# Heads' results kept features by tokens, with 32x32 turns on VectorE in place of TensorE's transposes

## The chip, the cores and the metric

One core of one Trainium2 chip. The metric is the device time of one execution in microseconds; lower is better. The kernel before has a median of 2641.17 us over three runs (2639.9 to 2641.59). Its profiled execution took 2642.54 us, of which the trace's span is 2640.5 us.

## The reference

x is 2048 tokens by 576 features in fp32. It is normalised, goes through an attention with 32 heads of 18 features and through a gated network with 4608 hidden units; the two results are multiplied and added to x.

```python
xn = _layernorm(x, axis=-1)
q, k, v = ...            # from xn @ wqkv, each heads x tokens x 18
scores = jnp.einsum("bhqd,bhkd->bhqk", q, k) * Dh ** -0.5
o = jnp.einsum("bhqk,bhkd->bhqd", softmax(scores), v)
s = o.transpose(0, 2, 1, 3).reshape(B, S, D) @ wo
gate, up = xn @ W_gate, xn @ W_up
g = silu(((gate * (gate > 0)) * up) @ W_down)
return x + s * g
```

## The kernel before

Most products are made in split fp32: each operand is a rounded high part and a low part, and three products are added. The contraction of these products uses 64 rows of TensorE at a time, so that two of them, on the upper and the lower 64 rows ("lanes"), run side by side. The class `Lanes` keeps a plan of both lanes, of eight PSUM banks and of VectorE ("V") and ScalarE ("A"), with fixed costs in microseconds, and hands out the matmuls in the order in which this plan would run them. A score matmul takes a bank when the plan has one free (`room`, `take`); `evict` books the bank's emptying on V or A; `hold` takes a bank for something else and `pause` moves both lanes on. TensorE's instructions keep that order; the other engines get theirs from the framework.

There are three stages.

- **Start** (to about 420 us): normalisation, q, k and v; the first hidden units.
- **Main loop** (about 420 to 2560 us): for each pair of heads `u` (16) four cycles `i`. A cycle runs two hidden units (`pg`, `pu`, `py`: gate, up, down), 32 score matmuls `psx` whose exponentials go through ScalarE, and 32 matmuls `pm` of the next pair of heads, whose row maxima VectorE takes (L383). Then `attend` multiplies 64 times with the values (`po`). After an odd cycle the two halves of `po` are added into `ot` (L855) and the pair of token halves is finished.
- **Projection** (last 80 us): for 16 tiles of 128 tokens, `heads` splits the attention's result into high and low parts, 28 matmuls `pw` multiply with `wo`, VectorE multiplies with the gate (L1046), GpSimd adds x (L1050), and SyncE stores.

Two things in the main loop are turned round by TensorE. `max_rows` (every 128x64 block of maxima `mx`) makes 128x32 values `nx` (maximum as high and low part), transposes them into a bank, copies them to `nt` on ScalarE and writes them with 8 DMAs as two extra rows into the q tiles `qT`, where the exponentials' matmuls subtract them. `finish_pair` (features on partitions: 18 of each 32 are a head's results, the 19th is the sum of its exponentials) transposes `ot` in four 128x128 blocks into a bank, after which VectorE takes the reciprocals `rc` (L786), multiplies into `ob` (L788, twice), and one DMA stores to `od`, tokens by features. Both wait in the list `tasks` until after the next even cycle's `attend`. In the projection `heads` transposes each tile of `od` back, in five 128x128 blocks (`tps`), so that features are on partitions; ScalarE and VectorE read these from PSUM (L991 to L997).

GpSimd meanwhile splits the weights (`gw`, `dw`, L295 and L296), in the projection it multiplies the gate (L971). All loads and stores of these stages go through SyncE's queue (SP), in the order in which the framework puts them.

Of the kernel before, what the change touches and what calls it, by code (L numbers as in the profile page):

```python
# [9 lines left out]
F32 = mybir.dt.float32  # L10
F32R = mybir.dt.float32r
AF = mybir.ActivationFunctionType
ALU = mybir.AluOpType
# [194 lines left out]
def kernel(  # L208
# [26 lines left out]
    HW = 2 * DH  # L235
# [3 lines left out]
    KA = 3 * DH  # L239
    C4 = 4 * P  # L240
    DT = D - C4
# [19 lines left out]
    def tp(*args):  # L261
        return keep(nc.tensor.transpose(*args))  # L262
# [20 lines left out]
    lanes = Lanes(8, bank, mm, fence)  # L283
# [62 lines left out]
    tasks = []  # L346
# [281 lines left out]
    two = pool(right, "two", 2, "right")  # L628
# [118 lines left out]
    def place_v(u):  # L747
        if u < NU:
            va, raw = vas[u % 2], raws.pop(u)
            for i in range(2):  # L750
                keep(nc.gpsimd.tensor_copy(va[:, :, i * VA : i * VA + DH], raw[:, :, i * DH : (i + 1) * DH]))

    def run_tasks(todo):
        for fn, args in todo:
            fn(*args)

    def max_rows(qs, mx):

        nm = two.tile([P, 2, 2, 4], F32, name="nm")
        nx = two.tile([P, 2, 2, 2, 4], F32, name="nx")  # L760
        nc.vector.tensor_reduce(nm, mx, axis=AX.X, op=ALU.max, negate=True)
        nxr = nx.bitcast(F32R)
        nc.scalar.activation(nxr[:, :, :, 0], nm, AF.Copy)
        nc.vector.tensor_tensor(nxr[:, :, :, 1], nm, nx[:, :, :, 0], ALU.subtract)
        b, ps = lanes.hold("tp")
# [3 lines left out]
        def write(ps):  # L769
            nc.scalar.activation(nt_.bitcast(F32R), ps[0:32, 0:P], AF.Copy)  # L770
            for q, qT in enumerate(qs):
                for h in range(2):
                    for a in range(2):
                        r = h * R + KA + a
                        p0 = q * 16 + h * 8 + a * 4
                        nc.sync.dma_start(
                            qT[r : r + 1, :].rearrange("o (j t) -> o j t", t=P).bitcast(F32), nt_[p0 : p0 + 4, :]
                        )

        lanes.evict(b, ps, lanes.pause(0.2), [("A", 0.27, write)])  # L780

    def finish_pair(ot, dst, then, *args):

        def write(ps):
            rc = two.tile([P, 16], F32, name="rc")
            nc.vector.reciprocal(rc, ps.rearrange("p (a d) -> p a d", d=32)[:, :, DH])  # L786
            for q in range(2):
                nc.vector.tensor_tensor(  # L788
                    dst[q].rearrange("p t (h d) -> p t h d", d=DH),
                    ps.rearrange("p (t h q d) -> p q t h d", h=2, q=2, d=32)[:, q, :, :, :DH],  # L790
                    rc.rearrange("p (t h q) -> p q t h", h=2, q=2)[:, q].unsqueeze(3).to_broadcast([P, 4, 2, DH]),
                    ALU.mult,
                )
            then(*args)

        def rest_():
# [36 lines left out]
    def attend(u, qp, done):  # L833
# [22 lines left out]
            done(qp, ot)  # L856

        lanes.evict(b, ps, end, [("V", 0.69, add)] if ots else [("A", 0.6, copy)])

    def to_dram(u):  # L860
        ob = two.tile([P, NT, HW], F32, name="ob", bufs=1)

        def store(qp):
            ts = slice(qp * NT // 2, (qp + 1) * NT // 2)
            nc.sync.dma_start(od[:, u * HW : (u + 1) * HW].rearrange("(t p) d -> p t d", p=P)[:, ts], ob[:, ts])

        return lambda qp, ot: finish_pair(
            ot, [ob[:, (2 * qp + q) * 4 : (2 * qp + q + 1) * 4, :] for q in range(2)], store, qp
        )

    def cycle(k, scores):

# [28 lines left out]
    for k in range(0, N1, 2):  # L901
        i = k // 2
# [15 lines left out]
    for u in range(NU):  # L918
        done = to_dram(u)
        pms = [maxima(u + 1, h) if u + 1 < NU else deque() for h in range(2)]  # L920
        for i in range(UN // 2):
# [9 lines left out]
            qp, k0 = i // 2, i % 2 * (NT // 2)  # L931
# [16 lines left out]
    fo = pool(fin, "fo", 4)  # L948
# [32 lines left out]
    def any_bank(name):  # L981
        turns[0] += 1
        return bank(turns[0] % 8, name)

    def heads(o):

        ps = any_bank("tps")
        for c in range(4):
            tp(ps[:, c * P : (c + 1) * P], o[:, c * P : (c + 1) * P], ident)
        hh = hp.tile([P, 2, 512], F32R, tag="hh", name="hf", bufs=4)  # L990
        nc.scalar.activation(hh[:, 0], ps, AF.Copy)  # L991
        nc.vector.tensor_tensor(hh[:, 1], ps, hh[:, 0].bitcast(F32), ALU.subtract)
        p5 = any_bank("tps")
        tp(p5[:, :P], o[:, C4:], ident)
        o5 = f2.tile([P, P], F32R, name="o5")
        nc.scalar.activation(o5, p5[:, :P], AF.Copy)
        nc.vector.tensor_tensor(o5[DT:P], p5[DT:P, :P], o5[DT:P].bitcast(F32), ALU.subtract)  # L997
# [15 lines left out]
    for j in range(4):  # L1013
        js = slice(j * P, (j + 1) * P)
        for n in range(2):
            cs = halves[n]
            ps = any_bank("py")[:, :HC]
# [5 lines left out]
    run_tasks(tasks)  # L1023
# [56 lines left out]
```

## Time and profile before

| | us | share of the span |
|---|---|---|
| median of three runs | 2641.17 | |
| profiled execution | 2642.54 | |
| its span | 2640.5 | 100% |
| TensorE matmuls busy | 2607.2 | 99% |
| VectorE busy | 1733.0 | 66% |
| ScalarE busy | 1464.0 | 55% |
| GpSimd busy | 1442.1 | 55% |
| transposes of `ot`, TensorE, 128 of 273 ns (overlapping) | 492.9 to 2566.7 | |
| transposes of `o` in the projection, 80 of 272 ns (overlapping) | 2566.9 to 2624.2 | |

PE is TensorE, PEld its weight loads, DVE VectorE, ACT ScalarE, POOL GpSimd, SP SyncE. Matmuls overlap in the pipeline, so the time that a group takes is read from the starts of what stands before and behind it, not from the durations. The granted TensorE clock is 1.00 in every stretch from 280 us on but the last 10.5 us (0.97).

### The profile page before, as it was taken

The page shows a single profiled execution, that of the slowest core. Times are in us where ns is not written, and L with a number is a line of the kernel's source. Part 1 is how long each engine was busy: PE and PEld are TensorE (multiplying, and loading weights), DVE is VectorE, ACT ScalarE, POOL GpSimd, SP SyncE. Part 2 cuts the span into 40 slices and gives each one's busy share as a digit, 9 for nine tenths or more (in the row PEclk, how much of TensorE's full clock was granted, in tenths as well). Part 3 has the DMA queues.
Part 4 walks back from the last instruction along what each step waited for, and adds up shares of the span by engine and source line. Part 5 has one row for each costly group of instructions (what it writes and reads, how often), then busy time and mean ns, then how long its engine had stood idle before and what let it go on. Part 6 is the DMA issues. An engine that isn't in the chain of part 4 may idle for free.

```text
span 2640.5 us, 62759 instructions
## 1 busy us (share of the span) xinstructions
PE 2607.2 (99%) x25436; PEld 2119.1 (80%) x25436; DVE 1733.0 (66%) x2888; ACT 1464.0 (55%) x2755; POOL 1442.1 (55%) x1273
## 2 busy tenths in 40 slices
PE   7998999999999999999999999999999999999999
PEld 5997887778887777777778778887777777778789
DVE  5325557777777777777777777777777777776124
ACT  2221226666666666666666666666666666666662
POOL 5234886555555555555555555555555555555555
PEclk9998999999999999999999999999999999999999
DMA  8644332222232222222242222222233222222247
GB/s 253 201 145 147 88 87 74 71 69 72 83 115 72 67 70 73 74 73 74 69 132 63 67 75 66 75 71 72 73 99 89 70 76 70 74 66 56 59 123 237
DMA packets 293265, 243.69 MB, mean 92 GB/s; under 512 B 64496, under 2 KB 236272, under 8 KB 292976
## 3 DMA queue, kind: packets, MB, share of 16 engines
q1 hardware_dynamic: 286192, 216.08, 28.2%
q0 software_dynamic: 6784, 23.60, 2.8%
q8 instruction: 201, 3.29, 0.5%
q14 instruction: 88, 0.72, 0.1%
HBM read 193.45 MB, written 45.61 MB: 91 GB/s over the span
## 4 chain that ended last, share of the span: by engine, by line
PE 93%; DMA 2%; POOL 2%; SPq 1%; DVE 1%; ACT 0%; issue 0%; POOLq 0%; ACTq 0%; DVEq 0%
PE pg L259 22%; PE po L259 17%; PE py L259 16%; PE pu L259 11%; PE pm L259 9%; PE psx L259 9%; PE pq L259 4%; PE pv L259 2%; PE pw L259 1%; PE tp L262 1%; SPq L353 1%; PE tps L262 1%; DMA rg<-in_B_W_up_dram 1%; DMA kT<-kd 1%; DMA gt<-yd 0%; DMA out_dram<-xr 0%
## 5 line engine op out<-in xcount | busy, mean ns | idle before, releaser
L383 DVE TENSOR_REDUCE mx<-pm 128x1 f32<-128x512 f32 x2048 | 1379.1, 689 | 254.4 <-PE pm L259 168.5
L817 ACT ACTIVATE p<-psx 128x512 f32<-128x512 f32 x2048 | 1182.3, 598 | 542.1 <-PE psx L259 258.8
L259 PE MATMUL pg<-x,gw 64*128 64x512 f32 x3888 | 1159.7, 392 | 5.7 <-POOL gw L296 3.7
L259 PE MATMUL pu<-x,gw 64*128 64x512 f32 x3888 | 1146.9, 392 | 0.0
L259 PE MATMUL pm<-kT,qT 54*128 54x512 f32 x2048 | 794.1, 398 | 3.0 <-DMA kT<-kd 3.0
L259 PE MATMUL psx<-qT,kT 56*128 56x512 f32 x2048 | 786.3, 394 | 0.0
L259 PEld LDWEIGHTS pg<-x,gw 64*128 64x128 f32 x3888 | 721.0, 187 | 60.5 <-POOL gw L296 4.6
L259 PEld LDWEIGHTS pu<-x,gw 64*128 64x128 f32 x3888 | 718.9, 187 | 25.0
L259 PE MATMUL py<-dw,hh 64*128 64x288 f32 x6864 | 717.5, 295 | 1.4 <-POOL dw L296 0.3
L259 PEld LDWEIGHTS py<-dw,hh 64*128 64x128 f32 x6864 | 662.8, 186 | 49.3 <-issue 30.1
L259 PE MATMUL po<-p,va 128*32 128x512 f32 x4096 | 452.7, 594 | 0.4 <-ACT p L817 0.4
L667 POOL CAST hh<-h 128x512 fp32r<-128x512 f32 x127 | 77.6, 611 | 612.3 <-DVE h L664 612.3
L694 POOL TENSOR_TENSOR y<-yt,y 128x288 f32<-128x288 f32 x268 | 215.2, 806 | 323.7 <-ACT yt L693 323.5
L259 PEld LDWEIGHTS psx<-qT,kT 56*128 56x128 f32 x2048 | 375.3, 185 | 18.9
L296 POOL TENSOR_TENSOR gw<-rg,gw 128x1152 fp32r<-128x1152 f32 x144 | 383.5, 2664 | 11.6
L259 PEld LDWEIGHTS pm<-kT,qT 54*128 54x128 f32 x2048 | 372.4, 185 | 18.5 <-issue 3.2
L259 PEld LDWEIGHTS po<-p,va 128*32 128x32 f32 x4096 | 126.4, 110 | 279.1 <-issue 269.1
L296 POOL TENSOR_TENSOR dw<-rd,dw 128x576 fp32r<-128x576 f32 x144 | 204.9, 1423 | 11.5
L670 POOL TENSOR_TENSOR hh<-h,hh 128x512 fp32r<-128x512 f32 x144 | 186.3, 1294 | 38.0 <-ACT hh L669 27.8
L295 POOL CAST gw<-rg 128x1152 fp32r<-128x1152 f32 x144 | 165.2, 1147 | 18.0 <-DMA rg<-in_B_W_up_dram 11.5
L689 DVE TENSOR_TENSOR y<-py,y 128x288 f32<-128x288 f32 x268 | 120.2, 449 | 49.5 <-PE py L259 48.9
L660 ACT ACTIVATE h<-pg 128x512 f32<-128x512 f32 x144 | 85.9, 597 | 116.7 <-PE pg L259 56.2
(80 smaller groups left out, 1353.0 us busy)
## 6 DMA issues: line engine op xcount, KB each, us to landing
rd<-in_B_W_down_dram SPq DMA_DIRECT2D x144, 288.0 KB
rg<-in_B_W_gate_dram SPq DMA_DIRECT2D x144, 256.0 KB
rg<-in_B_W_up_dram SPq DMA_DIRECT2D x144, 256.0 KB
qT<-qd SPq DMA_DIRECT2D x384, 36.0 KB
kT<-kd SPq DMA_DIRECT2D x384, 36.0 KB
kd<-hh POOLq DMA_DIRECT2D x16, 512.0 KB, 4.6
qd<-hh POOLq DMA_DIRECT2D x16, 512.0 KB, 5.7
xTd<-x SPq DMA_DIRECT2D x15, 512.0 KB
```

What stands on the lines that cost most here:

```text
L259: return keep(nc.tensor.matmul(*args, **kw))
L262: return keep(nc.tensor.transpose(*args))
L295: keep(nc.gpsimd.tensor_copy(hi, raw))
L296: keep(nc.gpsimd.tensor_tensor(lo, raw, hi.bitcast(F32), ALU.subtract))
L353: nc.sync.dma_start(dst[r0 : r0 + DH, :].bitcast(F32), src[i, f0 : f0 + DH, cs])
L383: nc.vector.tensor_reduce(mx[:, g % 2, h, j, c : c + 1], ps, axis=AX.X, op=ALU.max)
L660: nc.scalar.activation(made[0], ps, AF.Relu)
L667: keep(nc.gpsimd.tensor_copy(hh[:, 0], h))
L670: keep(nc.gpsimd.tensor_tensor(hh[:, 1], h, hh[:, 0].bitcast(F32), ALU.subtract))
L689: nc.vector.tensor_tensor(ys[j][:, cs], ps[:, :HC], ys[j][:, cs], ALU.add)
L694: keep(nc.gpsimd.tensor_tensor(ys[j][:, cs], t, ys[j][:, cs], ALU.add))
L817: nc.scalar.activation(p[0][:, h, i, :], ps, AF.Exp, scale=SCALE)
```

## The change

The heads' results stay features by tokens: `od` is now 576 x 2048. `to_dram` gives a `finish` that runs directly behind the add of the two halves: a 32x32 block transpose of `ot` on VectorE brings each block's 32 features onto the free axis, the reciprocals and the product are made there in place, a second block transpose turns the blocks back, and four DMAs store 18 rows of 512 tokens each. `max_rows` turns its 128x32 values in the same way, stores them to a small DRAM tile `nd`, and four DMAs read them back as rows. The plan no longer holds banks or pauses for these; it books 1.9 us on V for a finished pair, and 1.2 us on V and 0.25 us on A for the maxima. In the projection `load_heads` loads features by tokens, and `heads` splits straight from SBUF. TensorE transposes nothing but the normalised x in the start.

```diff
-    od = dram.tile([S, D], F32, name="od")
+    od = dram.tile([D, S], F32, name="od")
+    nd = dram.tile([2, 32, P], F32, name="nd")
...
-        b, ps = lanes.hold("tp")
-        tp(ps[0:32, 0:P], nx.rearrange("p q h a j -> p (q h a j)"), ident)
-        nt_ = two.tile([32, P], F32, name="nt")
...
-            nc.scalar.activation(nt_.bitcast(F32R), ps[0:32, 0:P], AF.Copy)
...
-        lanes.evict(b, ps, lanes.pause(0.2), [("A", 0.27, write)])
+        nt_ = two.tile([P, 32], F32, name="nt")
+        nc.vector.transpose(nt_, nx.rearrange("p q h a j -> p (q h a j)"))
+        lanes.server["V"] += 1.2
+        lanes.server["A"] += 0.25
+        n_ = nd[rows_kept[0] % 2]
+        rows_kept[0] += 1
+        nc.sync.dma_start(n_.rearrange("c (b t) -> b c t", b=4), nt_)
+        for q, qT in enumerate(qs):
+            for h in range(2):
+                r, p0 = h * R + KA, q * 16 + h * 8
+                nc.sync.dma_start(
+                    qT[r : r + 2, :].bitcast(F32), n_[p0 : p0 + 8, :].rearrange("(a j) t -> a (j t)", a=2)
+                )
-    def finish_pair(ot, dst, then, *args):
...
-            b, ps = lanes.hold("tp2")
-            for j in range(4):
-                tp(ps[:, j * P : (j + 1) * P], ot[:, j * P : (j + 1) * P], ident)
-            lanes.evict(b, ps, lanes.pause(0.6), [("V", 0.85, write)])
-        tasks.append((rest_, ()))
+    def to_dram(u):
+        def finish(qp, ot):
+            oT = two.tile([P, 512], F32, name="oT", bufs=1)
+            o3 = oT.rearrange("p (k d) -> p k d", d=32)
             rc = two.tile([P, 16], F32, name="rc")
+            nc.vector.transpose(oT, ot)
+            nc.vector.reciprocal(rc, o3[:, :, DH])
+            nc.vector.tensor_tensor(
+                o3[:, :, :DH], o3[:, :, :DH], rc.unsqueeze(2).to_broadcast([P, 16, DH]), ALU.mult
+            )
+            nc.vector.transpose(ot, oT)
+            lanes.server["V"] += 1.9
+            for h in range(2):
+                for i in range(2):
+                    s_ = 32 * (2 * h + i)
+                    f0, t0 = (2 * u + h) * DH, (2 * qp + i) * 512
+                    nc.sync.dma_start(od[f0 : f0 + DH, t0 : t0 + 512], ot[s_ : s_ + DH, :])
...
-        o = fo.tile([P, D + DT], F32, name="o")
-        nc.sync.dma_start(o[:, :D], od[k * P : (k + 1) * P, :])
-        nc.sync.dma_start(o[:, D:], od[k * P : (k + 1) * P, C4:])
+        o = fo.tile([P, 5, P], F32, name="o")
+        ks = slice(k * P, (k + 1) * P)
+        nc.sync.dma_start(o[:, :4], od[:C4, ks].rearrange("(c p) t -> p c t", p=P))
+        for d in range(2):
+            nc.sync.dma_start(o[d * DT : (d + 1) * DT, 4], od[C4:, ks])
...
-        ps = any_bank("tps")
-        for c in range(4):
-            tp(ps[:, c * P : (c + 1) * P], o[:, c * P : (c + 1) * P], ident)
+        o4 = o.rearrange("p c t -> p (c t)")[:, :512]
         hh = hp.tile([P, 2, 512], F32R, tag="hh", name="hf", bufs=4)
-        nc.scalar.activation(hh[:, 0], ps, AF.Copy)
-        nc.vector.tensor_tensor(hh[:, 1], ps, hh[:, 0].bitcast(F32), ALU.subtract)
+        nc.scalar.activation(hh[:, 0], o4, AF.Copy)
+        nc.vector.tensor_tensor(hh[:, 1], o4, hh[:, 0].bitcast(F32), ALU.subtract)
...
-        nc.vector.tensor_tensor(o5[DT:P], p5[DT:P, :P], o5[DT:P].bitcast(F32), ALU.subtract)
+        nc.vector.tensor_tensor(o5[DT:P], o[DT:P, 4], o5[DT:P].bitcast(F32), ALU.subtract)
```

What this does to the order of instructions is shown at three places. First VectorE, where an odd cycle of the main loop ends. Before:

```order
L761 TENSOR_REDUCE nm<-mx 128x16
L764 TENSOR_TENSOR nx<-nm,nx 128x4x4
L855 TENSOR_TENSOR ot<-po,ot 128x512
L383 TENSOR_REDUCE mx<-pm 128x1 x8
L689 TENSOR_TENSOR y<-py,y 128x288
```

And now (its line numbers are the changed kernel's):

```order
L767 TENSOR_TENSOR nx<-nm,nx 128x4x4
L769 STREAM_TRANSPOSE nt<-nx 128x32
L855 TENSOR_TENSOR ot<-po,ot 128x512
L789 STREAM_TRANSPOSE oT<-ot 128x512
L790 RECIPROCAL rc<-oT 128x16
L791 TENSOR_TENSOR oT<-oT,rc 128x16x18
L794 STREAM_TRANSPOSE ot<-oT 128x512
L384 TENSOR_REDUCE mx<-pm 128x1 x6
```

Four instructions now stand between the add and the first maximum of the next cycle; the reciprocal and two products that came one cycle later are gone from there.

Second TensorE, in the cycle behind that same place. Before, from the last product of attention on:

```order
L259 MATMUL po<-p,va_2826 32x512 x32
L259 MATMUL py<-dw,hh 128x288 x10
L259 MATMUL psx<-qT,kT_2428 128x512
L259 MATMUL pm<-kT_2436,qT 128x512
L259 MATMUL py<-dw,hh 128x288 x2
```

Now:

```order
L259 MATMUL po<-p,va_2827 32x512 x32
L259 MATMUL py<-dw,hh 128x288 x10
L259 MATMUL psx<-qT,kT_2429 128x512 x2
L259 MATMUL py<-dw,hh 128x288 x2
L259 MATMUL pg<-x,gw 128x512
L259 MATMUL pu<-x,gw 128x512
L259 MATMUL pg<-x,gw 128x512
L259 MATMUL pu<-x,gw 128x512
L259 MATMUL psx<-qT,kT_2429 128x512
L259 MATMUL pm<-kT_2437,qT 128x512
```

The plan sees VectorE taken and puts a second exponentials' matmul where the first `pm` stood; of the first 40 matmuls of 512 columns behind this place four are `pm`, where six were. Behind even cycles the five transposes are gone and the order is otherwise as it was.

Third SyncE's queue at the start of the projection. Before (`o`, `xr`, `gt` are the loads of a tile's heads, of x and of the gate's product):

```order
L968 DMA gt<-yd 128x576
L962 DMA o<-od 128x576
L963 DMA o<-od 128x64
L976 DMA xr<-in_A_x_dram 128x576
L968 DMA gt<-yd 128x576
L962 DMA o<-od 128x576
L1051 DMA out_dram<-xr 128x576
```

Now:

```order
L800 DMA od<-ot 18x512 x4
L731 DMA yd<-y 128x576 x3
L967 DMA xr<-in_A_x_dram 128x576
L959 DMA gt<-yd 128x576
L1036 DMA out_dram<-xr 128x576
L952 DMA o<-od 128x4x128
L954 DMA o<-od 64x128 x2
L967 DMA xr<-in_A_x_dram 128x576
L959 DMA gt<-yd 128x576
```

Before, the gate of tile 3 was asked for ahead of tile 0's store; now it stands behind that store, and so on for each tile: one tile less is loaded ahead. The two `gt` in each piece are those of tiles 2 and 3.

More of the change, by code (lines that the diff above doesn't have):

```diff
@@ L751, in place_v @@
                 keep(nc.gpsimd.tensor_copy(va[:, :, i * VA : i * VA + DH], raw[:, :, i * DH : (i + 1) * DH]))
+    rows_kept = [0]
     def run_tasks(todo):
@@ L764, in max_rows @@
         nc.vector.tensor_tensor(nxr[:, :, :, 1], nm, nx[:, :, :, 0], ALU.subtract)
-        b, ps = lanes.hold("tp")
-        tp(ps[0:32, 0:P], nx.rearrange("p q h a j -> p (q h a j)"), ident)
-        nt_ = two.tile([32, P], F32, name="nt")
-        def write(ps):
-            nc.scalar.activation(nt_.bitcast(F32R), ps[0:32, 0:P], AF.Copy)
[L771 to L778, printed above, removed]
@@ L780, in max_rows @@
-        lanes.evict(b, ps, lanes.pause(0.2), [("A", 0.27, write)])
-    def finish_pair(ot, dst, then, *args):
-        def write(ps):
-            rc = two.tile([P, 16], F32, name="rc")
[L786 to L796, printed above, removed]
-            b, ps = lanes.hold("tp2")
-            for j in range(4):
-                tp(ps[:, j * P : (j + 1) * P], ot[:, j * P : (j + 1) * P], ident)
-            lanes.evict(b, ps, lanes.pause(0.6), [("V", 0.85, write)])
-        tasks.append((rest_, ()))
+        nt_ = two.tile([P, 32], F32, name="nt")
@@ new lines, in to_dram @@
+    def to_dram(u):
+        def finish(qp, ot):
+            oT = two.tile([P, 512], F32, name="oT", bufs=1)
+            o3 = oT.rearrange("p (k d) -> p k d", d=32)
+            rc = two.tile([P, 16], F32, name="rc")
+            nc.vector.transpose(oT, ot)
[10 more added lines that the diff above has]
+                    nc.sync.dma_start(od[f0 : f0 + DH, t0 : t0 + 512], ot[s_ : s_ + DH, :])
+        return finish
@@ L858, in attend @@
         lanes.evict(b, ps, end, [("V", 0.69, add)] if ots else [("A", 0.6, copy)])
[L860 to L869, printed above, removed]
     def cycle(k, scores):
@@ L985, in heads @@
     def heads(o):
-        ps = any_bank("tps")
-        for c in range(4):
-            tp(ps[:, c * P : (c + 1) * P], o[:, c * P : (c + 1) * P], ident)
+        o4 = o.rearrange("p c t -> p (c t)")[:, :512]
         hh = hp.tile([P, 2, 512], F32R, tag="hh", name="hf", bufs=4)
-        nc.scalar.activation(hh[:, 0], ps, AF.Copy)
-        nc.vector.tensor_tensor(hh[:, 1], ps, hh[:, 0].bitcast(F32), ALU.subtract)
-        p5 = any_bank("tps")
-        tp(p5[:, :P], o[:, C4:], ident)
+        nc.scalar.activation(hh[:, 0], o4, AF.Copy)
+        nc.vector.tensor_tensor(hh[:, 1], o4, hh[:, 0].bitcast(F32), ALU.subtract)
         o5 = f2.tile([P, P], F32R, name="o5")
-        nc.scalar.activation(o5, p5[:, :P], AF.Copy)
-        nc.vector.tensor_tensor(o5[DT:P], p5[DT:P, :P], o5[DT:P].bitcast(F32), ALU.subtract)
+        nc.scalar.activation(o5, o[:, 4], AF.Copy)
+        nc.vector.tensor_tensor(o5[DT:P], o[DT:P, 4], o5[DT:P].bitcast(F32), ALU.subtract)
         return hh, o5
@@ L1022 @@
     store_y(last)
-    run_tasks(tasks)
     xts = {i: load_res(horder[i]) for i in range(2)}
```

## The prediction

> **What bounds the kernel now.** I read the busy shares first, then the chain of waits, then tables of stretches cut at the products of attention.
>
> ```profile
> PE 2607.2 (99%) x25436; PEld 2119.1 (80%) x25436; DVE 1733.0 (66%) x2888; ACT 1464.0 (55%) x2755; POOL 1442.1 (55%) x1273
> PE 93%; DMA 2%; POOL 2%; SPq 1%; DVE 1%; ACT 0%; issue 0%; POOLq 0%; ACTq 0%; DVEq 0%
> ...
> 459.07:485.84 26.77, 26.77 (x272) 24.80 (x268) 23.56 (x37) 20.09 (x37) 11.67 (x12) 1.00 0.24 69
> 485.84:493.50 7.66, 7.66 (x72) 2.45 (x71) 1.16 (x3) 0.86 (x3) 7.50 (x8) 1.00 0.25 68
> 493.50:520.27 26.77, 26.77 (x270) 24.47 (x269) 23.69 (x39) 20.69 (x38) 11.78 (x12) 1.00 0.27 73
> 520.27:527.27 7.00, 7.00 (x66) 1.97 (x64) 1.83 (x5) 0.81 (x3) 6.84 (x6) 1.00 0.35 96
> ```
>
> TensorE sets the end: 99% busy, 93% of the chain. The four rows are two cycles of the main loop (length; busy time of PE, PEld, DVE, ACT and POOL; clock; DMA share; GB/s). TensorE is busy in all of each row, so what leaves its queue there leaves the time, unless something new makes it wait. The third number after the length is the warning: VectorE works 23.6 of a cycle's 26.77 us. Its 66% is an average over stages; inside a cycle it is at 88%, and only during the products of attention does it rest.
>
> **What TensorE loses.** Both kinds of cycle from the start of the products of attention on:
>
> ```profile
> 452.07 7.07 PE L259 MATMUL po<-p,va 128*32 128x512 f32 x64
> 459.07 0.94 PE L259 MATMUL py<-dw,hh 64*128 64x288 f32 x10
> 459.84 0.39 PE L259 MATMUL psx<-qT,kT 56*128 56x512 f32 x1
> ...
> 485.84 7.07 PE L259 MATMUL po<-p,va 128*32 128x512 f32 x64
> 492.85 0.28 PE L262 MATMUL tp<-ident,nx 128*32 128x128 f32 x1
> 492.97 0.60 PE L262 MATMUL tp<-ident,ot 128*128 128x128 f32 x4
> 493.50 0.94 PE L259 MATMUL py<-dw,hh 64*128 64x288 f32 x10
> ```
>
> Behind an odd cycle 7.00 us pass from the first `po` to the first `py`; behind an even one, with five transposes, 7.66 us. So five transposes cost 0.66 us on TensorE, not the 1.4 us that their overlapping durations add up to. Of the 32 pairs of halves 31 are turned round in the loop: 31 x 0.66 = **20.5 us** off the path. The two sets of maxima before the loop bring 0.2 us more.
>
> **What VectorE gains, and who waits.** The finish of a pair moves from a place where VectorE rested (behind the transposes, 0.26 us of reciprocal and two products of 0.31 us) to directly behind the add of an odd cycle, where the next cycle's maxima queue up behind it. What it costs:
>
> ```profile
> L383 DVE TENSOR_REDUCE mx<-pm 128x1 f32<-128x512 f32 x2048 | 1379.1, 689 | 254.4 <-PE pm L259 168.5
> L689 DVE TENSOR_TENSOR y<-py,y 128x288 f32<-128x288 f32 x268 | 120.2, 449 | 49.5 <-PE py L259 48.9
> L786 DVE RECIPROCAL rc<-tp x32: 249/258/259, 493.6 to 2567.1; 128x16 f32<-128x16 f32 x32
> L788 DVE TENSOR_TENSOR ob<-tp,rc x64: 295/306/308, 493.9 to 2567.6; 128x144 f32<-128x144 f32 x64
> 459.21 0.69 DVE L855 TENSOR_TENSOR ot<-po,ot 128x512 f32<-128x512 f32 x1 [5.04 <-PE po L259]
> 460.30 0.69 DVE L383 TENSOR_REDUCE mx<-pm 128x1 f32<-128x512 f32 x1 [0.40 <-PE pm L259]
> 459.40 0.67 POOL L295 CAST dw<-rd 128x576 fp32r<-128x576 f32 x1
> 460.14 1.43 POOL L296 TENSOR_TENSOR dw<-rd,dw 128x576 fp32r<-128x576 f32 x1
> ```
>
> No block transpose of VectorE stands in this trace. The two group rows, 512 elements in 0.69 us and 288 in 0.45, give about 0.14 us fixed and 1.07 ns an element. If a turn passes one element a cycle it takes 0.69 us, which I use, since every fp32 pass over 512 columns here takes that; if it streams two at a time, 0.14 + 0.27 = 0.41; if it has to pass everything twice, 0.14 + 1.10 = 1.24.
>
> The product of 288 elements reads both operands from SBUF, and for that the trace shows a trap:
>
> ```profile
> 2633.02 1.43 POOL L1050 TENSOR_TENSOR xr<-xr,gt 128x576 f32<-128x576 f32 x1 [0.91 <-DVE gt L1046]
> 2633.34 1.43 DVE L1048 TENSOR_TENSOR xr<-xr,gt 128x288 f32<-128x288 f32 x1
> 2635.17 0.46 DVE L1048 TENSOR_TENSOR xr<-xr,gt 128x288 f32<-128x288 f32 x1
> ```
>
> The same instruction takes 0.46 us alone and 1.43 us when it meets GpSimd's: GpSimd's ends at 2634.45, and VectorE's, 0.32 us later, at 2634.77. It waited for GpSimd to end. [...]
>
> Now the finish, from the add's start at 459.21. Add to 459.90; first turn to 460.62; reciprocal to 460.9; then the product meets GpSimd's `dw`, which runs to 461.57, and is through at 461.9; second turn to 462.6. VectorE's first maximum starts there instead of at 460.30, 3.5 us into the cycle instead of 1.2. After that it has its old 23 us of work less 0.69 us of add, and its idle time in the cycle was 3.2 us, so the sum still fits (about 26 of 26.77). TensorE waits only where banks run out.
>
> Walk them: eight banks, four of them with the open accumulations (two `py`, `pg`, `pu`), four for scores. The changed order has its first four `pm` as 8th, 18th, 28th and 29th matmul of 512 columns. Twelve `py` take 0.92 us (ten are 0.77: 459.07 to 459.84), and two lanes of 512 columns pass in 0.234 us (the two starts below lie seven pairs apart), so they start at 1.7, 2.9, 4.1 and 4.2 us.
>
> ```profile
> 494.87 0.39 PE L259 MATMUL pg<-x,gw 64*128 64x512 f32 x1
> 496.51 0.39 PE L259 MATMUL pg<-x,gw 64*128 64x512 f32 x1
> ```
>
> The first bank is read out at 3.5 + 0.69 = 4.2 us and free just after. With one bank still held by a `psx`, the fourth `pm` waits 0.1 to 0.2 us; behind it VectorE stays late for the rest of the cycle and gives one bank each 0.69 us, so some later ones wait as well. I take **0.35 us** for a cycle. The lower end is 0, if banks happen to suffice; the upper is 1.0, from turns of 1.24 us (finish 0.5 us later still, as GpSimd's end covers the first turn's excess), a fourth `pm` 0.6 us late and some more behind it. 29 such cycles have `pm` (the last pair of heads has none to prepare): 29 x 0.35 = **10.2 us** given back, between 0 and 29.
>
> The maxima's turn (128x32) adds some 0.2 us, but it runs while TensorE is in `po` and VectorE rests; the rows are not read until a whole cycle later, 26 us, against two transfers of a few us, so their way through DRAM is hidden. SyncE waits for the first of them, but what stands behind it, the next `rg`, waits for GpSimd anyway. ScalarE loses a copy of 0.27 us, off the path. The stores are 2 KB rows instead of pieces of 144 bytes.
>
> **The projection.** TensorE's period for a tile, and what feeds it:
>
> ```profile
> 2566.48 0.60 PE L262 MATMUL tp<-ident,ot 128*128 128x128 f32 x4
> 2568.52 1.99 PE L259 MATMUL pw<-wo,hf 128*128 128x288 f32 x12
> ...
> 2602.26 0.71 PE L262 MATMUL tps<-ident,o 128*128 128x128 f32 x5
> 2602.72 1.83 PE L259 MATMUL pw<-wo,hf 128*128 128x288 f32 x12
> 2606.51 0.71 PE L262 MATMUL tps<-ident,o 128*128 128x128 f32 x5
> ...
> 2602.84 0.38 SPq L1051 DMA_DIRECT2D out_dram<-xr  x1
> 2603.31 0.38 SPq L968 DMA_DIRECT2D gt<-yd  x1
> 2607.34 0.69 ACT L970 ACTIVATE sg<-gt 128x576 f32<-128x576 f32 x1 [2.89 <-DMA gt<-yd]
> 2608.16 1.43 POOL L971 TENSOR_TENSOR gt<-gt,sg 128x576 f32<-128x576 f32 x1 [1.40 <-ACT sg L970]
> 2600.00:2610.00 10.00, 10.00 (x80) 10.00 (x79) 3.42 (x8) 2.19 (x5) 7.00 (x6) 1.00 0.91 292
> 2558.62 6.98 POOL L1006 TENSOR_TENSOR wo<-rw,wo 128x576 fp32r<-128x576 f32 x5
> L992 DVE TENSOR_TENSOR hf<-tps,hf x16: 679/691/693, 2568.2 to 2631.1; 128x512 fp32r<-128x512 f32 x16
> L997 DVE TENSOR_TENSOR o<-tps,o x16: 294/295/296, 2568.9 to 2631.8; 64x128 fp32r<-64x128 f32 x16
> ```
>
> A tile takes 4.25 us, of which the transposes are 0.46. Without them TensorE alone would need 3.79; 16 x 0.46 and the last pair's four transposes (0.4 us) would be 7.8 us. [...] The DMA share is 0.91, so a tile keeps the queues busy for 0.91 x 4.25 = 3.9 us, and `o` in rows of 512 bytes will not make that less. GpSimd's two instructions for a tile (2 x 1.43) and VectorE's two subtractions (0.69 and 0.29), which now read both operands from SBUF, exclude one another: 3.84 us. [...] I take 4.0 us, 0.25 less than now, over 13 tiles: 3.3 us.
>
> At the start the change loses some of it. VectorE does two `hf` subtractions before the last add, each behind one of GpSimd's five `wo` instructions (6.98 us in a row), and the last finish, so the first gate product, the first store and with it the gate of tile 3 come some 3 us later; TensorE itself starts its first `pw` 2 us earlier (2566.48 instead of 2568.52), since `hf` no longer waits for it. Net I count **0.5 us** gained for the stage, between 6 lost (4.5 us a tile and the late start) and 7.8 gained.
>
> **Sum**, against the profiled execution's 2642.54 us (1.4 above the median of 2641.17): -20.5 - 0.2 + 10.2 - 0.5 = -11.0, which from the median is **2630 us**.
>
> **Rivals.**
>
> *All of it arrives.* The banks suffice, or the turns take 0.41 us; the product still waits for GpSimd's 461.57, so the first maximum comes at 3.2 us. With 0.1 us a cycle and 3 us from the projection: -20.7 + 2.9 - 3 = -20.8, 2620. For it: VectorE's sum fits its cycle. Against: the fourth `pm`.
>
> [...]
>
> *VectorE becomes the bound of the main loop.* Its place is the finish, its price the turns. At 1.24 us each, 1.0 us a cycle: 29.0 given back against 20.7, and a projection 1 us worse: +9.3, 2650. It decides from 0.7 us a cycle on (20.5 / 29). For it: VectorE is at 88% in a cycle. Against: no fp32 instruction here passes its elements at half the rate. [...]
>
> *The turned results don't remove the transposes* can be left out: the order has none behind the start.
>
> **How the numbers follow.** This kernel's runs tell differences from about 0.2%, 5.3 us. Chances: the forecast 0.45, its own range 2623 to 2638; all of it arrives 0.15; the slower projection 0.21; VectorE as the bound 0.19. Faster by over 0.2% (below 2635.9) take the first (0.39 of its 0.45), the second and a little of the third (0.03): 0.57. Within 0.2%: 0.06, 0.16 of the third and 0.03 of the fourth: 0.25. Slower: the rest, 0.18. The range for 8 in 10 is 2617 to 2650.
>
> **What would show it.** Right: 7.00 us behind every cycle, even and odd; cycles behind even ones still at 26.77 us, those behind odd ones at about 27.1; the product of 288 elements at about 1 us, ending with GpSimd's `dw`; turns near 0.69 us. Wrong: turns above 1 us, an idle TensorE in front of `pm` with VectorE as the releaser for more than 0.7 us a cycle, or a projection longer than now from the last `py` to the end.

## The result, and the profile after

| | before | changed |
|---|---|---|
| median of 12 runs each, us | 2640.32 (2638.88 to 2643.78) | 2635.97 (2634.21 to 2637.14) |
| ratio, 95% interval | | 0.9983 (0.9974 to 0.9991) |
| profiled execution, its span, us | 2642.54, 2640.5 | 2636.32, 2634.5 |
| first `po` to the last half's `po`, us | 2134.71 | 2130.57 |
| first `py` behind the last `po` to the end ("the stage" below), us | 80.48 | 79.59 |

The change makes the kernel 4.35 us faster, 0.17%. The two spans lie 6.0 us apart: 4.14 in the loop, 0.96 ahead of it and 0.89 in the stage. From the page of the changed kernel, the busy shares:

```profile
PE 2595.1 (99%) x25196; PEld 2105.4 (80%) x25196; DVE 1796.8 (68%) x2952; ACT 1461.2 (55%) x2723; POOL 1446.8 (55%) x1273
```

TensorE has 240 instructions and 12 us of work less, VectorE 64 us more. TensorE is still busy for 99% of the span, so the page hides what happened. The table of stretches, divided as before the change, shows it (length; busy time of PE, PEld, DVE, ACT, POOL; clock; DMA share; GB/s):

```profile
451.12:458.12 7.00, 7.00 (x66) 1.97 (x64) 2.04 (x6) 0.81 (x3) 6.84 (x6) 1.00 0.29 78
458.12:485.49 27.37, 27.37 (x272) 24.64 (x268) 25.24 (x40) 20.35 (x37) 11.73 (x12) 1.00 0.31 88
485.49:492.50 7.01, 7.01 (x66) 1.98 (x66) 1.70 (x4) 0.41 (x1) 6.82 (x8) 1.00 0.21 64
492.50:519.31 26.81, 26.81 (x272) 25.61 (x268) 22.88 (x36) 20.72 (x38) 12.39 (x12) 1.00 0.23 67
```

Third row: the stretch with the five transposes fell from 7.66 to 7.01 us. Second row: the cycle behind an odd one, which now starts with the finish, grew from 26.77 to 27.37 us. The fourth is as it was. Over the whole loop the 31 shorter stretches bring 31 x 0.65 = 20.2 us; the 29 cycles behind odd ones average 27.32, so 29 x 0.55 = 16.0 us go back. That leaves 4.2, and the loop is 4.14 us shorter.

VectorE at the start of such a cycle, and GpSimd at the same time (start, duration, in brackets what ended the idle time before):

```profile
458.26 0.69 DVE L855 TENSOR_TENSOR ot<-po,ot 128x512 f32<-128x512 f32 x1 [4.78 <-PE po L259]
458.99 0.71 DVE L789 STREAM_TRANSPOSE oT<-ot 128x512 f32<-128x512 f32 x1
459.73 0.25 DVE L790 RECIPROCAL rc<-oT 128x16 f32<-128x16 f32 x1
460.02 0.94 DVE L791 TENSOR_TENSOR oT<-oT,rc 128x288 f32<-128x288 f32 x1
460.99 0.71 DVE L794 STREAM_TRANSPOSE ot<-oT 128x512 f32<-128x512 f32 x1
461.63 2.53 DVE L384 TENSOR_REDUCE mx<-pm 128x1 f32<-128x512 f32 x4
```

```profile
459.21 1.44 POOL L297 TENSOR_TENSOR dw<-rd,dw 128x576 fp32r<-128x576 f32 x1
```

The first maximum starts at 461.63, 3.51 us into the cycle. The product ran beside GpSimd's `dw` (to 460.65) and took 0.94 us. Four maxima follow one another without a gap. TensorE there, its matmuls and then its weight loads (PEld):

```profile
462.06 0.39 PE L259 MATMUL pg<-x,gw 64*128 64x512 f32 x1
462.34 0.50 PE L259 MATMUL pm<-kT,qT 54*128 54x512 f32 x2
462.67 0.39 PE L259 MATMUL pu<-x,gw 64*128 64x512 f32 x1
```

```profile
462.33 0.19 PEld L259 LDWEIGHTS pm<-kT,qT 54*128 54x128 f32 x2 [0.32 <-DVE mx L384]
462.93 0.18 PEld L259 LDWEIGHTS psx<-qT,kT 56*128 56x128 f32 x1 [0.30 <-DVE mx L384]
```

At 462.06 one lane starts a `pg` alone. The `pm` of the other lane, and the next, start at 462.34, that is 0.02 us after the first maximum has ended (461.63 + 0.69 = 462.32), and a maximum released their weight loads. The first of the two waited 0.28 us for a bank. Then TensorE waits a second time: the weights of the `psx` behind them are loaded at 462.93, 0.05 us after the end of the second maximum, which released them. This `psx` starts 4.81 us into the cycle; where nothing waits it starts at 4.41. Behind each wait the load starts together with its matmul (0.50 us instead of 0.39), and the next matmuls follow 0.33 us later instead of 0.23. Worked out from the starts of all matmuls, the cycle is about 0.3 us behind that of the kernel before at 4.5 us, 0.35 to 0.4 at 6 and 0.5 to 0.55 at 8, and hardly falls back further.

Not every such cycle lost that much. Of the 29, 25 have both waits and lost 0.53 to 0.67 us; four (the starts 799.00, 1343.90, 1411.56 and 2025.05) have neither and lost only 0.12 to 0.17. The first of them, VectorE and TensorE:

```profile
800.92 0.46 DVE L791 TENSOR_TENSOR oT<-oT,rc 128x288 f32<-128x288 f32 x1
801.41 0.71 DVE L794 STREAM_TRANSPOSE ot<-oT 128x512 f32<-128x512 f32 x1
802.05 2.64 DVE L384 TENSOR_REDUCE mx<-pm 128x1 f32<-128x512 f32 x4
```

```profile
802.94 0.63 PE L259 MATMUL pm<-kT,qT 54*128 54x512 f32 x2
803.41 0.43 PE L259 MATMUL psx<-qT,kT 56*128 56x512 f32 x1
```

In these four the `dw` did not run beside the product, which took 0.46 us instead of 0.94, and the first maximum started 3.05 us into the cycle. The first of the two `pm` started at 802.94, 3.94 us into the cycle, and the `psx` at 4.41, with no wait. So the trace already suggests that VectorE's lateness costs nothing up to a point. The `pm` are held up when the first maximum starts later than 3.25 us (3.94 less the 0.69 of a maximum). The `psx` comes 1.30 us behind the start of the first maximum when it waits (4.81 less 3.51), so it is held up earlier, from about 3.1 us on (4.41 less 1.30, an estimate).

### The profile page after: what moved, and what is told of

Read it like the earlier page. It is cut to its first block, busy times and chain, and to the rows that moved or that the text cites. A ratio compares the mean times of both kernels' runs of the same rounds, so it can differ in the third digit from the quotient of the medians.

```text
span 2634.5 us, 62653 instructions
## 1 busy us (share of the span) xinstructions
PE 2595.1 (99%) x25196; PEld 2105.4 (80%) x25196; DVE 1796.8 (68%) x2952; ACT 1461.2 (55%) x2723; POOL 1446.8 (55%) x1273
## 5 line engine op out<-in xcount | busy, mean ns | idle before, releaser
L384 DVE TENSOR_REDUCE mx<-pm 128x1 f32<-128x512 f32 x2048 | 1364.2, 688 | 401.5 <-PE psx L259 202.0
L259 PE MATMUL pu<-x,gw 64*128 64x512 f32 x3888 | 1134.5, 392 | 0.0
L259 PE MATMUL pm<-kT,qT 54*128 54x512 f32 x2048 | 773.4, 398 | 4.3 <-DMA qT<-qd 2.8
L259 PE MATMUL psx<-qT,kT 56*128 56x512 f32 x2048 | 774.5, 396 | 0.0
L259 PE MATMUL py<-dw,hh 64*128 64x288 f32 x6864 | 737.9, 296 | 1.9 <-DVE ot L855 0.4
L259 PEld LDWEIGHTS py<-dw,hh 64*128 64x128 f32 x6864 | 672.2, 186 | 71.7 <-issue 50.3
L259 PEld LDWEIGHTS psx<-qT,kT 56*128 56x128 f32 x2048 | 369.4, 185 | 23.9 <-DVE mx L384 3.1
```

The costliest lines, as they stand in the source:

```text
L259: return keep(nc.tensor.matmul(*args, **kw))
L384: nc.vector.tensor_reduce(mx[:, g % 2, h, j, c : c + 1], ps, axis=AX.X, op=ALU.max)
```

## The experiments

**Theory and rivals.** Theory: the finish makes VectorE late, and TensorE waits for banks. Rivals: the planner's new order (it books 1.9 us of VectorE and so moves `pm` back) costs the time itself; or another engine does.

**One more turn.** Behind the second turn:

```diff
             nc.vector.transpose(ot, oT)
+            o2 = two.tile([P, 512], F32, name="o2", bufs=1)
+            nc.vector.transpose(o2, oT)
```

> The changed kernel with one turn of 512 columns more behind the second, into a tile that nobody reads, and not booked with the planner: same order of TensorE, VectorE 0.71 us later in 32 cycles. Theory (VectorE's lateness decides, and the lateness was past the point from which it costs): about 0.7 us more in each of the 29 cycles behind odd ones that prepare maxima, 27.4 -> 28.1, total +17 to +20 us, about 2655. Rival (the 0.6 us come from the order, or from another engine): 0 to +3 us, those cycles stay at 27.4.

2651.52 us (ratio to before 1.0039, 1.0025 to 1.0053), 15.6 above the changed kernel; cycles behind odd ones 27.99 us, 0.61 more than the changed kernel's 27.38 (medians). VectorE and TensorE in such a cycle:

```profile
457.53 0.67 DVE L796 STREAM_TRANSPOSE o<-oT 128x512 f32<-128x512 f32 x1
458.12 2.53 DVE L384 TENSOR_REDUCE mx<-pm 128x1 f32<-128x512 f32 x4
```

```profile
457.98 0.39 PE L259 MATMUL pg<-x,gw 64*128 64x512 f32 x1
458.83 0.50 PE L259 MATMUL pm<-kT,qT 54*128 54x512 f32 x2 [0.46 <-DVE mx L384]
```

The first maximum comes 4.08 us into the cycle, 0.57 later than in the changed kernel, and the `pm` pair starts 0.02 us after its end (458.12 + 0.69 = 458.81). The theory holds, though both numbers stay a little under its range: the turn moved the first maximum by 0.57 us, not 0.71.

**No product.** The product between the turns is left out, and with it the division:

```diff
-            nc.vector.tensor_tensor(
-                o3[:, :, :DH], o3[:, :, :DH], rc.unsqueeze(2).to_broadcast([P, 16, DH]), ALU.mult
-            )
```

> The changed kernel without the product of 288 elements between the two turns (the division of the heads' results is left out; nothing else). [...] Theory (lateness decides): cycles behind odd ones 27.4 -> 26.8 to 26.9 us, total -12 to -17 us, about 2621. Rival (order or another engine): 27.4 stays, total within 2 us of 2636.

2623.42 us (0.9936, 0.9923 to 0.9950); cycles behind odd ones 26.91 us, first maximum at 2.36 us into the cycle. The theory holds. The 0.14 us that stay over 26.77 are there although VectorE is in time: in the first 7 us of these cycles no matmul waits for a maximum. I put them down to the planner's order (the rival has this much); the order alone, without any finish, was not run.

**No booking.**

```diff
-            lanes.server["V"] += 1.9
+            lanes.server["V"] += 0.0
```

> The changed kernel with one number changed: the planner books 0 us of VectorE for the finish instead of 1.9, so that behind an odd cycle's results the pm matmuls of the next cycle keep the early places that they have before the change (eight or nine maxima ahead of the first y add instead of six). Theory (VectorE's lateness decides): the finish takes 2.6 us whatever is booked, the earlier pm fill the banks sooner, TensorE waits longer in the first 8 us; cycles behind odd ones 27.4 -> 27.9 to 28.5 us, total +14 to +30 us. Rival (the planner's new order itself costs the 0.6 us, not VectorE): those cycles go back to 26.8, total -16 us, about 2620. Cycles behind even ones 26.8 and every stretch of po 7.00 in both.

2662.57 us (1.0086, 1.0072 to 1.0100), cycles behind odd ones 28.30 us. TensorE:

```profile
457.75 0.40 PE L259 MATMUL psx<-qT,kT 56*128 56x512 f32 x1
458.69 0.49 PE L259 MATMUL pm<-kT,qT 54*128 54x512 f32 x1 [0.54 <-DVE mx L384]
```

The third `pm` stands at 2.55 us again and waits until 3.48; 0.39 us follow at the fourth. The booking thus saves 0.92 us a cycle for the 0.14 that it costs, and the rival falls. The last stretch of `po` did not stay at 7.00 us: the first `py` behind it came 3.1 us late, as in the next run.

**The finish where VectorE rests.** The finish of a pair goes behind the last `y` add of the next cycle, with two `ot` tiles and no booking (in part):

```diff
-            attend(u, qp, done)
+            if i % 2 == 0 and unfinished:
+                with tc.issue_after(latest[0].ins):
+                    run_tasks([unfinished.pop()])
+            attend(u, qp, lambda *args, done=done: unfinished.append((done, args)))
```

> The changed kernel with the finish (turn, reciprocal, product, turn, four stores) put one cycle later: behind the last y add of the next cycle, where VectorE rests while TensorE is in that cycle's po (about 6.6 us, in which it only makes the maxima's rows); two ot tiles instead of one, nothing booked, so that the pm keep their early places; the last pair is finished at once as now. Theory (VectorE's lateness decides): cycles behind odd ones 27.4 -> 26.8 us, those behind even ones stay 26.8 (the finish of 2.6 us ends inside the 7.00 us of po), total -16 to -17 us, about 2619. Rival (order or another engine costs the 0.6): less than 4 us gained. A third way: the finish is not through before the next cycle's first pm, and the loss moves to the cycles behind even ones; total about 2636.

2621.21 us (0.9928, 0.9914 to 0.9941). Two rows of stretches, the cycle behind an odd one and the stretch that now holds the finish, and VectorE there:

```profile
455.88:482.66 26.78, 26.78 (x273) 25.17 (x269) 23.56 (x37) 20.12 (x37) 11.68 (x12) 1.00 0.24 71
482.66:489.67 7.01, 7.01 (x68) 1.97 (x66) 3.19 (x7) 0.59 (x2) 6.85 (x8) 1.00 0.33 94
```

```profile
484.75 0.46 DVE L791 TENSOR_TENSOR oT<-oT,rc 128x288 f32<-128x288 f32 x1
485.24 0.71 DVE L794 STREAM_TRANSPOSE ot<-oT 128x512 f32<-128x512 f32 x1
490.88 0.69 DVE L384 TENSOR_REDUCE mx<-pm 128x1 f32<-128x512 f32 x1 [4.93 <-PE pm L259]
```

The finish is through 4.9 us before VectorE is wanted, and the loop is 2114.50 us long: 20.2 less than before, all that the transposes had cost. The theory holds, with one miss: 3.2 us were lost again at the loop's end, where without the booking the first bank of the last `py` was that of the last `po`, whose reading stood behind two `hf` subtractions on VectorE:

```profile
2529.63 7.07 PE L259 MATMUL po<-p,va 128*32 128x512 f32 x64 [0.38 <-ACT p L816]
2539.90 5.35 PE L259 MATMUL py<-dw,hh 128*128 128x288 f32 x27 [3.20 <-DVE ot L854]
```

The four kernels, and the cycles with a shorter wait for `dw` in two of them, give one curve:

| | first maximum, us into the cycle | cycle behind an odd one, us | over 26.77 |
|---|---|---|---|
| finish at rest (early order) | 1.23 | 26.78 | 0.01 |
| no product | 2.36 | 26.91 | 0.14 |
| changed, four cycles (product 0.46) | 3.03 to 3.06 | 26.89 to 26.94 | 0.12 to 0.17 |
| changed, the cycle from 730.90 on | 3.37 | 27.30 | 0.53 |
| changed (median) | 3.48 | 27.38 | 0.61 |
| one turn more, four cycles (product 0.46) | 3.62 to 3.65 | 27.44 to 27.55 | 0.67 to 0.78 |
| one turn more (median) | 4.08 | 27.99 | 1.22 |

It is flat from 2.36 to 3.05 us, at the 0.14 of the order. Behind that it follows the later of the two waits: the `psx` starts 0.38 us late in the changed kernel and 0.97 with one turn more (4.79 and 5.38 instead of 4.41, medians), and some 0.1 us come on top (0.61 - 0.14 - 0.38 = 0.09; 1.22 - 0.14 - 0.97 = 0.11). That is as much as one weight load that starts together with its matmul costs (0.33 less 0.23); that it is this is not shown.

**The maxima's rows alone**, on the kernel before (the `max_rows` of the diff, nothing else):

> The kernel before with only the maxima's rows changed: their turn of 128x32 on VectorE and the way through DRAM; the heads' results still by TensorE's four transposes, and the projection as before. Theory (the rows' turn lies where VectorE rests, and TensorE's five transposes in front of the next cycle fall by one): the even stretches of po 7.66 -> 7.53 us, the cycles stay 26.77 behind even and odd ones, total -4 us (31 x 0.13) against the kernel before. Rival (the stretch pays for the stop, not for each transpose, or the rows' way costs on SyncE): 7.60 or more, total -2 to +2 us.

2639.06 us (0.9995, 0.9986 to 1.0004): by the runs alone not to be told from no change. The stretch:

```profile
483.57:491.16 7.59, 7.59 (x70) 2.40 (x68) 1.16 (x3) 0.61 (x2) 7.43 (x8) 1.00 0.24 69
```

7.59 us instead of 7.66, and the cycles stay at 26.77. So the narrow fifth transpose was worth 0.07 us, half of my expectation, and the four wide ones, with whatever the stop itself costs, the other 0.59. That lies at the rival's end, and so does the total, 1.5 us below the kernel before. The loop is 2.35 us shorter, 31 x 0.07 = 2.2, so the rows' way through DRAM costs nothing there.

**The projection.** In the changed kernel a tile takes 4.18 us in the steady part. VectorE and GpSimd:

```profile
2593.81 0.82 DVE L1031 TENSOR_TENSOR gt<-pw,gt 128x288 f32<-128x288 f32 x2 [1.33 <-POOL gt L962]
2595.26 1.40 DVE L983 TENSOR_TENSOR o<-o,o 64x128 fp32r<-64x128 f32 x1
2597.99 0.82 DVE L1031 TENSOR_TENSOR gt<-pw,gt 128x288 f32<-128x288 f32 x2 [1.33 <-POOL gt L962]
```

```profile
2594.76 1.74 POOL L1035 TENSOR_TENSOR xr<-xr,gt 128x576 f32<-128x576 f32 x1 [0.99 <-DMA gt<-yd]
2596.47 1.48 POOL L962 TENSOR_TENSOR gt<-gt,sg 128x576 f32<-128x576 f32 x1
```

Read as a ring: VectorE's products end at 2594.63, GpSimd adds x to 2596.50, multiplies the next gate to 2597.95, and VectorE starts at 2597.99. My theory was that this ring sets the period. Two tries to break it:

```diff
-            if i + 2 >= NT:
-                nc.vector.tensor_tensor(xt[:, cs], xt[:, cs], gt[:, cs], ALU.add)
-        if i + 2 < NT:
-            nc.gpsimd.tensor_tensor(xt, xt, gt, ALU.add)
+            nc.vector.tensor_tensor(xt[:, cs], xt[:, cs], gt[:, cs], ALU.add)
```

> The changed kernel with the projection's addition of x on VectorE for all 16 tiles (now the last two only), so that GpSimd has one instruction per tile instead of two. Theory (in the changed kernel a tile's 4.18 us are a ring over one tile: VectorE's two gate products 0.82, then GpSimd's addition 1.74, then GpSimd's gate product of the next tile 1.48, then VectorE again): the ring is cut, the period falls to 3.8 to 3.9 us, TensorE's own 3.79, VectorE's o5 subtraction goes from 1.40 back to 0.3 to 0.5; the stage from the last py of the cycles to the end is 79.6 -> 75 to 76 us, total -4 us. Rival (the transfers, busy for 0.95 to 0.97 of that stage, set the period): 4.1 to 4.2 us stays, total within 1 us of the changed kernel.

2636.29 us (0.9980, 0.9971 to 0.9989), no gain over the changed kernel; the stage took 82.3 us. GpSimd now waits, and what for:

```profile
2597.09 1.43 POOL L962 TENSOR_TENSOR gt<-gt,sg 128x576 f32<-128x576 f32 x1 [4.83 <-ACT sg L961]
```

```profile
2596.33 0.69 ACT L961 ACTIVATE sg<-gt 128x576 f32<-128x576 f32 x1 [2.24 <-DMA gt<-yd]
```

The gate's load is late, as the rival with the transfers has it. The tiles come unevenly, two at 3.6 to 3.9 us and two at about 5. The 82.3 us are of an execution that was the slowest of eleven (2638.95 us) and in which the granted clock was 0.50 for 3.4 us of the stage; the same additions gave 79.0 us in the best version below. The second try pinned the orders (each store one tile later on SyncE, GpSimd's gate product of tile i+2 ahead of the addition of tile i):

```diff
-        nc.sync.dma_start(out2[k * P : (k + 1) * P, :], xt)
+        if i:
+            keep(nc.sync.dma_start(out2[late[0] * P : (late[0] + 1) * P, :], late[1]))
+        late = k, xt
```

> The changed kernel with the projection's orders on GpSimd and SyncE written out: GpSimd multiplies the gate of tile i+2 before it adds x for tile i (now that of i+1 after it), and SyncE issues each store one tile later, behind the loads of the next gate. Same work. Theory (the ring over one tile between VectorE and GpSimd sets the 4.18 us): with the gate product two tiles ahead VectorE no longer waits for GpSimd (1.32 us a tile now), period 3.8 to 4.0, total -2 to -4 us. [...]

2647.47 us (1.0030, 1.0020 to 1.0040): worse than expected, with a stage of 91.4 us. The pinned order made a longer ring: a store (issued 2599.98), the next gate's load behind it on SyncE (2603.06), its sigmoid (2606.30), GpSimd's product (2607.12), and only then the addition (2608.51) that the store of 2609.96 waits for. That is 9.98 us for two tiles.

**Two limits side by side?** The new theory was that ring and transfers both stand near 4.1 us. Fewer transfers, with and without the additions on VectorE (`load_res`, x for twelve of the 16 tiles left out):

```diff
+        if len(kept_x) == 4:
+            kept_x.append(kept_x.pop(0))
+            return kept_x[-1]
```

> The changed kernel with x loaded for the first four tiles of the projection only, and these four buffers used again by the other twelve (the residual of these twelve tiles is left out: wrong rows are added): 288 of 1184 KB less per tile, GpSimd's two instructions a tile as now. Theory (after the run with the additions on VectorE: transfers and the ring VectorE-GpSimd both stand near 4.1 us a tile, and taking one away leaves the other): 4.18 us stays, within 1.5 us of the changed kernel's 79.6 for the stage. Rival (the transfers alone set the period, the ring only follows them): 3.7 to 3.9 us a tile, the stage 4 to 6 us shorter.

> The same, and the additions of x on VectorE for all tiles (residual of twelve tiles left out as in the run before it). Theory (two limits side by side): with both gone TensorE's own 3.72 us sets the period, PE idle behind hf falls from 0.7 to 1.5 us in single tiles to nothing, the stage takes 73 to 76 us instead of 82.3 with the additions alone. [...]

With fewer transfers alone the stage took 83.3 us (2639.05 us in all; 0.9991, 0.9982 to 1.0000), with both 76.4 (2630.76; 0.9956, 0.9941 to 0.9971). In the first a tile takes 4.84 us at a DMA share of only 0.63, since `hf` and `o5` had come to stand between VectorE's two gate products, so that the ring holds them too:

```profile
2591.74 0.46 DVE L1037 TENSOR_TENSOR gt<-pw,gt 128x288 f32<-128x288 f32 x1 [2.98 <-POOL gt L962]
2592.11 0.68 DVE L986 TENSOR_TENSOR hf<-o,hf 128x512 fp32r<-128x512 f32 x1
2592.83 0.29 DVE L989 TENSOR_TENSOR o<-o,o 64x128 fp32r<-64x128 f32 x1
2593.15 0.46 DVE L1037 TENSOR_TENSOR gt<-pw,gt 128x288 f32<-128x288 f32 x1
2596.58 0.46 DVE L1037 TENSOR_TENSOR gt<-pw,gt 128x288 f32<-128x288 f32 x1 [2.98 <-POOL gt L962]
```

With both gone TensorE runs without a stop over whole stretches of 10 us:

```profile
2591.00:2601.00 10.00, 10.00 (x78) 10.00 (x77) 9.28 (x17) 3.20 (x7) 2.87 (x2) 1.00 0.75 231
```

So neither edit alone gains anything, and both together gain 5.5 us against the additions alone (2636.29 to 2630.76, the medians); the stage's 76.4 us lie just above the 73 to 76 expected. That the ring would stay at 4.18 was wrong, and the run with fewer transfers alone is no clean test of the ring, since VectorE's order changed with it. Nor do these runs separate the amount of the transfers from the place of the gate's load in SyncE's queue: fewer loads of x change both.

**The best version.** The finish at rest, the additions on VectorE, and `turns[0] = b` in `attend`, so that the last `po`'s bank comes last among the projection's:

> The changed kernel with the finish one cycle later where VectorE rests (as in the run before that had only this, 2621), the projection's additions of x on VectorE, and the last stretch of po in the bank that comes last in the row of the projection's banks, so that the last py need not wait for its readout (in that run the bank fell first in the row: 3.20 us idle). Theory: cycles 26.77 and stretches of po 7.00 throughout, 16 us less than the changed kernel from there, 0.4 instead of 3.2 us idle behind the last po, a tile in 3.8 to 3.9 us: 2612 to 2615. Rival (the savings at the end overlap because the transfers of the projection set its end): 2617 to 2620.

**2618.54 us (0.9920, 0.9907 to 0.9934)**, 17 us below the changed kernel and 22 below the kernel before. The loop takes 2114.73 us, the 3.20 us behind the last `po` are gone, and the stage stays at 79.0: the total is the rival's, and the expectation's gain in the projection is the part that failed. A last try was to load x eight tiles ahead instead of two:

> The version of 2618.5 us (finish one cycle later, additions on VectorE, the last bank) with the projection's x loaded eight tiles ahead instead of two (ten buffers instead of four), so that six tiles of x come while the transfers are busy 0.67 to 0.74, and the steady tiles' transfers lose 288 of 1184 KB for the first half of the stage. Theory (the transfers set the projection's period once the ring is cut): the stage 79.0 -> 75 to 77 us, total 2614 to 2616. Rival (not the transfers, or the gate of the third tile is late behind seven loads of x): 2618 to 2621.

2623.94 us (0.9933, 0.9920 to 0.9945), stage 81.8: worse than either expected, by the mechanism of the second rival. The gate of the third tile is asked for behind seven loads of x, and ScalarE waits for it:

```profile
2561.49 0.68 ACT L964 ACTIVATE sg<-gt 128x576 f32<-128x576 f32 x1 [11.65 <-DMA gt<-yd]
```

TensorE stood still for 3.05 us, and in the 6.89 us behind the granted clock (last but two) was 0.56:

```profile
2563.95:2570.84 6.89, 6.17 (x26) 5.82 (x27) 6.76 (x12) 2.42 (x6) 2.87 (x2) 0.56 0.82 257
```

At the rate of 2551.40 to 2553.27 (14 matmuls in 1.87 us) its 26 matmuls would take 3.5 us. So some 6 of the 81.8 us are this stop and what followed it, an estimate, and the run leaves open whether the transfers set the period of the later tiles.

## Why the prediction was right, and where it was off

*Sign and reach.* 2635.97 lies 6 us above the forecast, 2630. The slower projection, to which the chances gave 0.21, did not come: the stage took 79.59 us instead of 80.48. The gain is 4.35 us of the 11 forecast; at 0.17% it falls by a hair among the changes within 0.2%, to which the prediction gave 0.25. That both large terms were right in kind is no luck; that the total is still inside the forecast's own range of 2623 to 2638 owes something to the width of that range.

*TensorE's transposes, 20.5 us.* Right: 7.00 us behind every cycle, and the version with the finish at rest has all of it (20.2). The run with the rows alone shows how it divides: 2.2 for the maxima, 18 for the heads.

*The turn, 0.69 us.* Right; a turn of 1.24 us, which "VectorE becomes the bound" needed, did not come:

```profile
L789 DVE STREAM_TRANSPOSE oT<-ot x32: 711/711/715, 459.0 to 2558.7; 128x512 f32<-128x512 f32 x32
L791 DVE TENSOR_TENSOR oT<-oT,rc x32: 458/918/1530, 460.0 to 2560.2; 128x288 f32<-128x288 f32 x32
```

Durations are the shortest, middle and longest in ns. The 1.24 was the author's estimate for passing everything twice (0.14 + 1.10), and no run shows it. A turn of 512 columns took 711 ns, a maximum over 512 in the same kernel 688 (mean of 2048).

*The first maximum 3.5 us into the cycle, behind a product of about 1 us that waits for GpSimd.* Right in both (3.51; middle 0.918 us).

*0.35 us a cycle, 10.2 us in all.* This is the term that was mis-sized: 0.62 us on average in 25 cycles, 0.12 to 0.17 in four, 16.0 us in all. The step: "with one bank still held by a `psx`, the fourth `pm` waits 0.1 to 0.2 us". In the trace already the third `pm` waits, 0.28 us: the walk put its start at 4.1 us, and where nothing waits it is at 3.94. "Some later ones wait as well" came true for one matmul, the `psx` that waits for the second maximum and starts 0.4 us late; behind 8 us hardly more is lost. The 0.14 of the planner's order I had not counted. The term stayed inside its bounds of 0 to 1.0. The walk had the collision with `dw` in its times, but not what it costs by itself. The finish ends only 0.4 us beyond the point up to which it is free (3.51 less 3.1), and the collision is 0.48 us of its length: without it about 29 x 0.14 = 4 us would have been lost instead of 16. That is read from four cycles (and four with one turn more, which also lost less); a version that avoids the collision and keeps the place was not tried.

*"All of it arrives"* needed the first maximum before about 3.1 us, where the curve bends; it put it at 3.2 us, and it came at 3.51.

*The projection, 0.5 us gained at 4.0 us a tile.* Measured 0.9 and 4.18 us. The 4.0, like the 4.5 of the lower bound, was the author's estimate, above the 3.9 of the transfers and the 3.84 of VectorE and GpSimd in turn; no run shows what it adds to them. In its place the runs showed a ring over one tile, GpSimd's two instructions (1.74 and 1.48 us) and VectorE's products (0.82). VectorE and GpSimd did hold one another up in it: `o5` took 1.40 us beside GpSimd's addition, and 0.29 with fewer transfers, where it ran clear of it; the addition took 1.74, and 1.43 there. But kernels with the same code in this stage take 79.6, 80.1 and 80.8 us (the changed kernel and the ones with a turn more and without the product), and 80.5 and 82.1 (the kernel before and with the rows alone); where 3 us were lost just ahead of the stage it is 78.4 and 79.5 (no booking, finish at rest). So neither 0.5 nor 0.9 is more than the spread.

*The start.* 418.30 and 417.34 us to the first `po`; among kernels with the same code up to there it is 413.25 to 417.8, so the 0.2 us of the early maxima can't be read.

## What to carry to other kernels

Moving work from a full engine to one that looks free pays by where the work lands: the same finish on VectorE cost 0.6 us a cycle directly behind a hand-over and 0.01 one stretch later. Work out the latest time at which the first results are wanted, the second as well as the first (here 4.41 us less 1.30 and 3.94 less 0.69), since up to it lateness cost nothing more here (0.14 us a cycle with the first maximum at 2.36 us and at 3.05) and behind it all of it was paid (0.61 at 3.48, 1.22 at 4.08). And where two limits seem to stand close together, as in the projection here, an edit that removes one can show nothing (2636.29 and 2639.05 us against the changed kernel's 2635.97, with both 2630.76); try both at once before either is called harmless.

## What the runs showed of the hardware that was not expected

- A turn of 128x512 on VectorE took 711 to 715 ns the first time of a pair and 695 to 715 the second in all 32, also while GpSimd was running; the product with two operands from SBUF took 458 to 1530 ns in the same place. In these 32 only the product was held up.
- The narrow one of TensorE's five transposes (32 columns of maxima) was worth 0.07 us (7.66 to 7.59), the four wide ones, with whatever the stop itself costs, 0.59 (7.59 to 7.00): counted by number alone it would have been 0.13.
- Where a matmul of the changed kernel waited for a bank (462.34 and 462.93), its weight load waited as well: it started with the matmul (462.33 and 462.93), the matmul shows 0.49 to 0.50 us instead of 0.39, and the next matmuls followed 0.33 to 0.34 us later instead of 0.23.
- TensorE stood still for 3.05 to 3.20 us in three runs (no booking, finish at rest, x early). In all three the granted clock was 0.50 for 3.4 to 6.9 us from about the end of the stop on (x early: 0.56 over the 6.89 us behind it). Of the shorter stops in the projections, up to 1.7 us, only one was followed by it (1.51 us, additions on VectorE).
